# FFN, Q and output matmuls behind a P V block issued as four 32-column tiles, with a planner that follows the tiling mode

## The chip, the cores and the metric

One core of one Trainium2 chip. The metric is the device time of one execution, in microseconds (us), as the median of several runs. "The profile" is one further execution taken by the hardware profiler; its span is the time from the first to the last instruction.

## The reference

A transformer layer on x of 2048 rows by 1024: layer norm, attention with 32 query heads of 32 and a single key/value head, residual; layer norm, gated FFN of width 3584, residual. All in bf16.

```python
q = (xn @ wq).reshape(S, 32, 32); k = xn @ wk; v = xn @ wv      # xn = layernorm(x)
p = softmax(einsum("hqd,kd->hqk", q, k) * 32 ** -0.5)
h = x + (p @ v).reshape(S, 1024) @ wo
g = hn @ w_gate; u = hn @ w_up                                  # hn = layernorm(h)
out = h + (sigmoid(g) * u) @ w_down
```

## The kernel before

**Attention.** Queries are cut into 16 tiles of 128 rows, heads into 8 blocks of four; a "group" G is one query tile with two head blocks (64 groups in all). A *visit* is one group with 256 keys: there are 512, eight a group, 32 a query tile. A visit does S (`emit_S`): eight matmuls of 32 contraction rows by 128, in four row tiles, over 256 columns, into three PSUM banks pairs in turn; then two exps on ScalarE (`ACT Pr L588`), each over 128x1024, which write the P slots of SBUF. After four visits of a group comes half of P V (`mk_PV`, `emit_PV`): 32 matmuls as four column tiles, 128 contraction rows by 32 columns each. The sums of P that softmax divides by are made in one of two ways. For the first four groups (`G < NX`) TensorE multiplies every P slot by ones, 32 more column-tiled matmuls a half. For all others VectorE adds the P slots up into `Ts` (`flush_sums`, L618), merges two halves (L625), and four matmuls with ones close the sum.

**The rest.** Q (`mk_Q`), the output projection (`mk_OP`), gate/up (`mk_GU`, 8 matmuls over 512 columns a group of 512 FFN columns) and down (`mk_D`) use the full 128x128 array. They are cut into single matmuls and stand between the S of two visits. Gate/up ends in a tanh on ScalarE (L860) for the sigmoid, and a multiply on VectorE (L864). Gate/up weights are streamed in pieces of 256 KB through 22 slots (`ring`) over SP's queue; down weights stay in SBUF (`zone`), where x transposed and wq lay before.

**What sets the order.** The kernel is written out by a planner in Python (`Plan`). It holds a free time for each engine and durations for each operation, and issues, one after the other: S as soon as ScalarE's backlog is under 750 ns, a P V block if its inputs are known, else a full matmul from the queues in the order `PRIO`. Where nothing is ready and a PSUM bank is spare, it issues a matmul that only fills the time (`F_ps<-kT,ident`); before visit 0 such matmuls warm up the engine (`S_ps<-hact,ident`). Constants for a change of tiling mode (95, 111, 109 ns) are added to TensorE's free time in `emit_S`, `emit_PV` and the main loop. On the chip each engine runs its own list in order, and semaphores hold it where inputs are late. All matmuls but the transposes come from the helper `mm` and so have one line, L384 in the profile; they are told apart by their tiles: `S_ps<-QTb,kT` is S, `F_ps<-Pr,Vb` P V, `F_ps<-Ts,ones` and `F_ps<-Pr,ones` its sums, `F_ps<-zone` Q, K and V, `F_ps<-wo_sb,OT` output, `F_ps<-ring,hnT` gate/up, `F_ps<-zone,hact` down.

**The start.** x tiles are loaded on SP's queue, wk and wv on ScalarE's. VectorE and GpSimd normalise pairs of x tiles; TensorE transposes the first two, DMAs the others. `TP` is the order of (query tile, FFN slice): slices of tiles 0 and 1 are interleaved by hand, later tiles go through the slices forwards and backwards in turn.

Of the kernel before, what the change touches and what calls it, by code (L numbers as in the profile page):

```python
# [128 lines left out]
def bass_sequential_preLN__grouped_kv_mqa__glu_gated_glu__prompt_kernel(  # L129
# [21 lines left out]
    NI = 2 * NFP  # L151
    TP = [(0, p) for p in range(5)] + [(1, 4), (1, 3), (0, 5), (1, 5), (0, 6), (1, 6)] + [(1, p) for p in (2, 1, 0)]
    TP += [(t, p) for t in range(2, NT) for p in (reversed(range(NFP)) if t % 2 else range(NFP))]
    ITEMS = [(t, p, w) for t, p in TP for w in range(2)]
# [6 lines left out]
    NPS = 16  # L161
    NX = 4
    NB = 3
    NPC = 22
# [8 lines left out]
    with ExitStack() as es:  # L173
# [43 lines left out]
        def xnT(dt, a, n):  # L217
            return xnT4[a // 512][:, dt, a % 512:a % 512 + n]
        wq_sb = zview(DT * S, DT, D)
        o3 = DT * S + DT * D  # L220
# [73 lines left out]
        def load_wq(a, b, deps=()):  # L294
            o = dma(lambda: SP.dma_start(wq_sb[:, :, a * P:b * P], A_wq[:, a * P:b * P].rearrange("(a p) n -> p a n", p=P)),
                    f"wq{a}", D * P * (b - a) * 2, deps, prio=0)
            for g in range(a, b):
                wq_ld[g] = o

        load_x([0])  # L300
        load_x([1])
        wk_ld = dma(lambda: ACT.dma_start(wk_sb, A_wk.rearrange("(a p) j -> p a j", p=P)), "wk", P * DT * DH * 6, prio=0,
                    ring="act")
        wv_ld = dma(lambda: ACT.dma_start(wv_sb, A_wv.rearrange("(a p) j -> p a j", p=P)), "wv", P * DT * DH * 6, prio=0,
                    ring="act")
        load_wq(0, 2)
# [76 lines left out]
        def mm(o, l, r, start, stop, **kw):  # L383
            return lambda: PE.matmul(o, lhsT=l, rhs=r, start=start, stop=stop, **kw)  # L384

# [45 lines left out]
        q_left4 = [2 * NG, 2 * NG, NG, NG]  # L431
        wd_ld = []

        def mk_KV(p):
# [27 lines left out]
        def mk_Q(g, tok, n):  # L462
            def atoms(b):
                return [(mm(F_ps[:, b, 0:n], wq_sb[:, dt, g * P:(g + 1) * P], xnT(dt, tok, n),
                            dt == 0, dt == DT - 1), n, []) for dt in range(DT)]

            def after(b, last):
                q_left[0] -= 1
                q_left4[tok // 512] -= 1
                free_wd(last)  # L470
                early_loads(last)
                if tok == 0:
                    fa, fd = both(QTb[:, :, g, :], F_ps[:, b, 0:256].rearrange("p (a b) -> p a b", a=2))
                    ev = evac(fa, fd, 256, [last], 1)
                    q_ready[0][g] = q_ready[1][g] = ev
                else:
                    k = len(q_store)
                    s = k % NQS
                    deps = [last] + ([q_store[k - NQS]] if k >= NQS else [])
                    fa, fd = both(qst[:, s, 0:n], F_ps[:, b, 0:n])  # L480
                    ev = evac(fa, fd, n, deps, 1)
                    q_store.append(dma(lambda: SP.dma_start(q_dram[:, g, tok:tok + n], qst[:, s, 0:n]),
                                       f"qs{s}", P * 2 * n, [ev], prio=2))
                    for t in range(tok // P, (tok + n) // P):
                        q_of[t].append(q_store[-1])
                        load_q(t)
                return [ev]
            first = lambda: [wq_ld[g]] + [xT_ev[k] for k in range(tok // P, (tok + n) // P)]
            return Group("Q0" if tok == 0 else "Q", atoms, first, after)
# [20 lines left out]
        def free_wd(last):  # L510
            for i in list(wd_left):
                if (i < 4 and q_left4[i] == 0 and 2 * i in k_ev and 2 * i + 1 in k_ev) or \
                        (i >= 4 and q_left[0] == 0 and len(k_ev) == NT // 2):
                    wd_left.remove(i)
                    load_wd(4 * i, 4, [last])
# [39 lines left out]
        def reclaim(v):  # L555
            for sl, own in list(slot_owner.items()):
                if own in pv_done and (own[0] < NX or slot_add.get(sl) is not None):
                    slot_rel[sl] = [pv_done[own], slot_add.get(sl)]
                    del slot_owner[sl]
                    p_free.append(sl)  # L560
            if visits[v][0] >= NX:
                for sl in [sl for sl in p_free if sl >= NPS]:
                    p_free.remove(sl)

        def emit_S(v):
            G, kq = visits[v]
            qb, g = G // ND, 2 * (G % ND)
            deps = s_ready(v)
            pl.free["pe"] += 95.0
            last = None  # L570
            for kk in range(KB):
                for j in range(4):
# [5 lines left out]
                                 deps if (kk == 0 and j == 0) else [], occ=27.4, lat=27.4 + 150.0 + SEM)  # L578
            pl.free["pe"] += 111.0
            for i in range(2):  # L580
# [21 lines left out]
        sum_ev = {}  # L602
        sum_todo = collections.deque((G, kq) for G in range(NX, NT * ND) for kq in range(1, VPG))

        def flush_sums():
            while sum_todo:
                G, kq = sum_todo[0]
                if n_exp_of[G] <= kq or (kq == 1 and G > NX + 1 and (G - 2, 1) not in pv_done):
                    return
                sum_todo.popleft()  # L610
                for i in range(2):
                    T = Ts[:, G % 2, i * 1024:(i + 1) * 1024]
                    ins = [kq - 1, kq] if kq == 1 else [kq]
                    src = [pslot(slot_of[(G, q, i)]) for q in ins]
                    deps = [exp_of[(G, q, i)] for q in ins]
                    deps.append((pv_done.get((G - 2, 1)) if G > NX + 1 else None) if kq == 1 else sum_ev[(G, kq - 1, i)])
                    a, b = (src[0], src[1]) if kq == 1 else (T, src[0])
                    o = pl.op("dve", lambda T=T, a=a, b=b: DVE.tensor_tensor(out=T, in0=a, in1=b, op=ALU.add), deps,  # L618
                              prio=4, **t_dve(1024, 1.92))
                    for q in ins:  # L620
                        slot_add[slot_of[(G, q, i)]] = o
                    sum_ev[(G, kq, i)] = o
# [10 lines left out]
        def mk_PV(G, h):  # L633
            qb, g = G // ND, 2 * (G % ND)

            def block(b):
                r, rs = [], []
                k0, k1 = 8 * h, 8 * h + 8
                for kt in range(k0, k1):
                    kq, kk = kt // KB, kt % KB  # L640
                    for j in range(4):
# [3 lines left out]
                                    kt == k0, kt == k1 - 1, tile_position=(0, DH * j)))  # L645
                        if G < NX:
                            rs.append(mm(F_ps[DH * j:DH * (j + 1), b, 256:512], ones[:, :], pslot(slot)[:, co:co + 256],
                                         kt == k0, kt == k1 - 1, tile_position=(0, DH * j)))
                for j in range(4 if G >= NX and h else 0):
                    r.append(mm(F_ps[DH * j:DH * (j + 1), b, 256:512], ones[:, :],  # L650
                                Ts[:, G % 2, j * 512:j * 512 + 256], True, True, tile_position=(0, DH * j)))
# [46 lines left out]
            def first():  # L698
                r = [exp_of[(G, kq, i)] for kq in range(VPH * h, VPH * (h + 1)) for i in range(2)]
                r += [v_ev.get(p) for p in range(4 * h, 4 * h + 4)]  # L700
                return r + [c_v1] + ([merge_ev.get(G)] if G >= NX and h else [])

# [4 lines left out]
        def emit_PV(t):  # L707
# [8 lines left out]
            b = min(banks, key=lambda b: max([0.0] + [o.end for o in bank_rel[b]]))  # L716
            deps = gr.first() + list(bank_rel[b])
            for fn in gr.atoms(b):
                o = pl.op("pe", fn, deps, occ=27.4, lat=27.4 + 220.0 + SEM)
                o.tag = "PV"  # L720
                deps = []
            pl.free["pe"] += 109.0
            bank_rel[b] = gr.after(b, o)
# [42 lines left out]
        def flush_hT():  # L766
            while late_hT and (late_hT[0] < 2 or (late_hT[0] - 2) in gu_last):
# [4 lines left out]
                for i in range(len(ITEMS)):  # L772
                    if ITEMS[i][0] == t if t > 1 else (ITEMS[i][0] < 2 and t == 0):
                        queues["GU"].append(mk_GU(i))
# [146 lines left out]
        while True:  # L921
# [15 lines left out]
            if sd is None and queues["PV"]:  # L937
                pl.free["pe"] += 95.0
                if emit_PV(t):
                    idle = 0  # L940
                    continue
                pl.free["pe"] -= 95.0
            if cur is not None:
                fn, n, deps, *cb = cur[1][cur_i]
                if known(deps, t) or not can_s:
                    o = pl.op("pe", fn, deps + (cur[2] if cur_i == 0 else []), **t_mm(n))
                    o.tag = cur[0].cls
# [33 lines left out]
            if v == 0 and known([c_id, c_w], t):  # L981
                pl.op("pe", mm(S_ps[:, 5, :], ident[:, :], hact[:, 0:512], True, True), [c_id, c_w], **t_mm(512))
                continue
            idle += 1
            spare = [b for b in range(2) if known(bank_rel[b], t) and (cur is None or b != cur_b)]
            if v and spare:
                pl.op("pe", mm(F_ps[:, spare[0], 0:256], ident[:, :], kT4[:, 0:256], True, True), [k_ev[0]] + list(bank_rel[spare[0]]), **t_mm(256))
                continue
# [108 lines left out]
```

The softmax here doesn't subtract the row's maximum and nothing guards it: scores larger than these inputs give would overflow.

## Time and profile before

| | us |
|---|---|
| median of 6 runs | 1109.46 (1107.73 to 1110.3) |
| the profiled execution, its own time | 1109.09 |
| its span | 1107.0 |
| first S starts, last S starts | 18.86, 1025.80 |

Of the groups of instructions these are the largest on each engine:

| line, engine, tiles | count | busy us, mean ns |
|---|---|---|
| L588 ACT Pr<-S_ps | 1014 | 952.1, 1058 |
| L618 DVE Ts<-Ts,Pr | 720 | 476.3, 681 |
| L384 PE F_ps<-ring,hnT 128x512 | 1754 | 439.7, 381 |
| L384 PE F_ps<-zone,hact 128x512 | 896 | 224.5, 381 |
| L384 PE S_ps<-QTb,kT 32x256 | 4096 | 203.3, 273 |
| L384 PE F_ps<-Pr,Vb 128x256 | 4056 | 134.5, 274 |
| L860 ACT tnh<-F_ps | 112 | 71.7, 640 |

A matmul's length in the profile is a modelled one and overlaps its neighbours; the distance from one start to the next is what it takes of the engine. "PE" is TensorE's matmuls, "PEld" its weight loads, "DVE" VectorE, "ACT" ScalarE, "SP" the DMA queue's engine.

### The profile page before, as it was taken

What the parts mean: (1) busy time and instruction counts of PE and PEld (TensorE: products, weight loads), DVE (VectorE), ACT (ScalarE), POOL (GpSimd) and SP (SyncE); (2) the same over time, 40 slices, a digit from 0 to 9 for tenths busy, and PEclk for the clock granted to TensorE, in tenths of its full rate; (3) what the DMA queues carried; (4) which work ended last, traced back from release to release, by engine and by line L of the source; (5) the groups of instructions that cost most, each with busy time, mean ns of one, the idle gap of its engine ahead of it and who ended that gap; (6) DMA issues with size and microseconds to landing.
All of it is one profiled execution on the core that took longest, in us unless ns stands there. A gap on an engine that the chain in (4) does not pass through costs nothing.

```text
span 1107.0 us, 30139 instructions
## 1 busy us (share of the span) xinstructions
PE 1090.1 (98%) x12306; PEld 475.0 (43%) x12306; DVE 884.7 (80%) x1727; ACT 1012.1 (91%) x1162; POOL 27.9 (3%) x56
## 2 busy tenths in 40 slices
PE   9999999999999999999999999999999999999998
PEld 5664344344344444444444444444444444344443
DVE  7747988798888989798888988898888888888411
ACT  4999999999999999999999999999999999999210
POOL 1100000000000000000000000000000000000000
PEclk9999999999999999999999999999999999999999
DMA  9985499928759595987869495976868595976991
GB/s 238 187 272 173 105 250 283 273 56 233 206 142 251 143 254 134 252 202 182 245 147 248 143 251 146 243 210 186 232 155 241 138 261 150 239 202 169 270 269 44
DMA packets 304730, 222.06 MB, mean 201 GB/s; under 512 B 121552, under 2 KB 295888, under 8 KB 304592
## 3 DMA queue, kind: packets, MB, share of 16 engines
q1 hardware_dynamic: 302512, 220.01, 77.8%
q8 instruction: 97, 1.59, 0.6%
q14 instruction: 41, 0.34, 0.1%
q10 hardware_dynamic: 2080, 0.13, 0.1%
HBM read 189.66 MB, written 7.86 MB: 178 GB/s over the span
## 4 chain that ended last, share of the span: by engine, by line
PE 88%; ACT 4%; DVE 4%; issue 2%; DMA 1%; SPq 0%; POOL 0%; POOLq 0%; DVEq 0%
PE F_ps L384 74%; PE S_ps L384 15%; ACT Pr L588 4%; DMA ring<-in_B_w_gate_dram 1%; DVE st L325 1%; DMA ring<-in_B_w_up_dram 0%; DVE st L323 0%; DVE Ts L618 0%; DVE ring L371 0%; DVE ring L364 0%; ACT tnh L860 0%; DVE hact L274 0%; DVE Rc L680 0%; DVE Oc L668 0%; DVE mv L327 0%
## 5 line engine op out<-in xcount | busy, mean ns | idle before, releaser
L588 ACT ACTIVATE Pr<-S_ps 128x1024 bf16<-128x1024 f32 x1014 | 952.1, 1058 | 6.8 <-PE S_ps L384 6.0
L618 DVE TENSOR_TENSOR Ts<-Ts,Pr 128x1024 bf16<-128x1024 bf16 x720 | 476.3, 681 | 41.2 <-ACT Pr L588 37.4
L384 PE MATMUL F_ps<-ring,hnT 128*128 128x512 bf16 x1754 | 439.7, 381 | 8.1 <-issue 2.2
L384 PEld LDWEIGHTS F_ps<-ring,hnT 128*128 128x128 bf16 x1754 | 149.8, 98 | 221.6 <-issue 79.1
L384 PE MATMUL F_ps<-zone,hact 128*128 128x512 bf16 x896 | 224.5, 381 | 0.0
L384 PE MATMUL S_ps<-QTb,kT 32*128 32x256 bf16 x4096 | 203.3, 273 | 0.2 <-DVE mv L327 0.2
L384 PEld LDWEIGHTS S_ps<-QTb,kT 32*128 32x128 bf16 x4096 | 60.6, 92 | 192.1 <-ACT Pr L588 131.2
L384 PE MATMUL F_ps<-Pr,Vb 128*32 128x256 bf16 x4056 | 134.5, 274 | 0.0
L864 DVE SCALAR_TENSOR_TENSOR hst<-tnh,F_ps 128x512 bf16<-128x512 f32 x112 | 76.7, 684 | 62.7 <-PE F_ps L384 62.7
L384 PEld LDWEIGHTS F_ps<-zone,hact 128*128 128x128 bf16 x896 | 76.2, 98 | 103.8 <-issue 32.4
L384 PEld LDWEIGHTS F_ps<-Pr,Vb 128*32 128x32 bf16 x4056 | 96.8, 96 | 36.7 <-DVE hst L864 10.9
L860 ACT ACTIVATE tnh<-F_ps 128x512 f32<-128x512 f32 x112 | 71.7, 640 | 44.6 <-PE F_ps L384 44.6
L618 DVE TENSOR_TENSOR Ts<-Pr 128x1024 bf16<-128x1024 bf16 x120 | 80.7, 688 | 37.4 <-ACT Pr L588 37.3
L384 PE MATMUL F_ps<-zone 128*128 128x256 bf16 (+2 forms) x576 | 76.2, 276 | 3.7 <-DVE mvb L333 1.0
L384 PE MATMUL F_ps<-wo_sb,OT 128*128 128x512 bf16 x256 | 63.6, 380 | 0.0
L384 PEld LDWEIGHTS F_ps<-zone 128*128 128x128 bf16 x576 | 42.6, 97 | 29.3 <-issue 8.9
L894 DVE SCALAR_TENSOR_TENSOR h_sb<-F_ps,h_sb 128x512 bf16<-128x512 f32 x32 | 22.0, 686 | 35.3 <-PE F_ps L384 35.3
L625 DVE TENSOR_TENSOR Ts<-Ts 128x1024 bf16<-128x1024 bf16 x60 | 41.4, 689 | 1.5
L337 POOL TENSOR_SCALAR zb<-mvb 128x1 bf16<-128x1 bf16 (+1 forms) x24 | 10.5, 439 | 1010.7 <-DVE mvb L333 1010.7
L384 PEld LDWEIGHTS F_ps<-wo_sb,OT 128*128 128x128 bf16 x256 | 22.4, 98 | 29.3 <-issue 6.8
L685 DVE STREAM_TRANSPOSE Rc<-Ri 128x256 f32<-128x256 f32 x64 | 28.3, 442 | 0.1
L668 DVE TENSOR_TENSOR Oc<-F_ps,Oc 128x256 f32<-128x256 f32 x60 | 25.2, 421 | 3.5 <-PE F_ps L384 2.3
(59 smaller groups left out, 350.4 us busy)
## 6 DMA issues: line engine op xcount, KB each, us to landing
ring<-in_B_w_gate_dram SPq DMA_DIRECT2D x308, 256.0 KB, 3.9
ring<-in_B_w_up_dram SPq DMA_DIRECT2D x307, 256.0 KB, 4.1
zone<-in_B_w_down_dram SPq DMA_DIRECT2D x28, 256.0 KB, 4.0
h_sb<-in_A_x_dram SPq DMA_DIRECT2D x16, 256.0 KB, 5.1
out_dram<-h_sb SPq DMA_DIRECT2D x32, 128.0 KB, 2.6
ring<-in_A_x_dram SPq DMA_DIRECT2D x7, 512.0 KB, 6.5
QTb<-q_scratch SPq DMA_DIRECT2D x14, 256.0 KB, 4.4
Pr<-in_B_w_up_dram SPq DMA_DIRECT2D x9, 256.0 KB, 3.8
```

Source lines behind the costliest of these rows:

```text
L325: b = pl.op("dve", lambda k=k, src=src: DVE.bn_stats(st[:, k, 1, :], src[:, 512:1024]), dep, prio=prio, occ=590, lat=756, order=[st_user.g ...
L337: f = pl.op("pool", lambda: POOL.tensor_scalar(out=zb[:, ph, sl].unsqueeze(2), in0=mvb[:, ph, sl, 1:2], scalar1=LN_EPS_BF16, scalar2=None, ...
L384: return lambda: PE.matmul(o, lhsT=l, rhs=r, start=start, stop=stop, **kw)
L588: exps[u] = pl.op("act", lambda slot=slot, pb=pb: ACT.activation(out=pslot(slot).rearrange("p (a b) -> p a b", a=2), in_=S_ps[:, pb:pb + 2 ...
L618: o = pl.op("dve", lambda T=T, a=a, b=b: DVE.tensor_tensor(out=T, in0=a, in1=b, op=ALU.add), deps, prio=4, **t_dve(1024, 1.92))
L625: merge_ev[G] = pl.op("dve", lambda T4=T4: DVE.tensor_tensor(out=T4[:, :, 0, :], in0=T4[:, :, 0, :], in1=T4[:, :, 1, :], op=ALU.add), [sum ...
L668: a = pl.op("dve", lambda: DVE.tensor_tensor(out=Oc[:, :], in0=O, in1=Ob, op=ALU.add), [last, oc_ev[G], o_ev.get(G - 1)], prio=0, **t_dve( ...
L685: d = pl.op("dve", lambda: DVE.transpose(out=Rc[:, :], in_=Ri[:, :].unsqueeze(2).to_broadcast([P, 2 * P // DH, DH])), [r], prio=2, **t_dve ...
L860: tanh_of[n] = pl.op("act", lambda: ACT.activation(out=tnh[:, n % 2, :], in_=F_ps[:, b, :], func=ACTF.Tanh, scale=0.5), [last, tn_user.get ...
L864: e = pl.op("dve", lambda: DVE.scalar_tensor_tensor(out=hst[:, n % NST, :], in0=tnh[:, n % 2, :], scalar=1.0, in1=F_ps[:, b, :], op0=ALU.a ...
L894: e = pl.op("dve", lambda: DVE.scalar_tensor_tensor(out=h_sb[:, t % 4, sl], in0=F_ps[:, b, :], scalar=0.5, in1=h_sb[:, t % 4, sl], op0=ALU ...
```

## The change

The planner keeps the tiling mode that TensorE is in (`mode`), and adds the drain where the mode changes (`enter`). A full matmul that comes while the mode is still that of P V goes out as four column tiles, up to `NCR` = 12 of them after one P V block:

```diff
+    NCR = 12
         def mm(o, l, r, start, stop, **kw):
-            return lambda: PE.matmul(o, lhsT=l, rhs=r, start=start, stop=stop, **kw)
+            fn = lambda: PE.matmul(o, lhsT=l, rhs=r, start=start, stop=stop, **kw)
+            if not kw:
+                fn.col = lambda: [mm(o[DH * j:DH * (j + 1)], l[:, DH * j:DH * (j + 1)], r, start, stop,
+                                     tile_position=(0, DH * j)) for j in range(4)]
+            return fn
+        mode = ["full"]
+        col_run = [0]
+        DRAIN = {"full": 96.0, "row": 92.0, "col": 100.0}
+        def enter(m):
+            if mode[0] != m:
+                pl.free["pe"] += DRAIN[mode[0]]
+                mode[0] = m
+                col_run[0] = 0
+        def emit_mm(fn, n, deps):
+            if mode[0] == "col" and hasattr(fn, "col") and col_run[0] < NCR:
+                col_run[0] += 1
+                for f in fn.col():
+                    o = pl.op("pe", f, deps, occ=n / 9.6 + 1.2, lat=n / 9.6 + 171.0 + SEM)
+                    deps = []
+                return o
+            enter("full")
+            return pl.op("pe", fn, deps, **t_mm(n))
...
-                    o = pl.op("pe", fn, deps + (cur[2] if cur_i == 0 else []), **t_mm(n))
+                    o = emit_mm(fn, n, deps + (cur[2] if cur_i == 0 else []))
```

`emit_S` calls `enter("row")` and adds 18 in place of 95 and 111; `emit_PV` calls `enter("col")` and adds 9 in place of 109.

The second half of the first four groups has its sums made by VectorE, as the later groups have:

```diff
-                        if G < NX:
+                        if h == 0 and G < NX:
                             rs.append(mm(F_ps[DH * j:DH * (j + 1), b, 256:512], ones[:, :], pslot(slot)[:, co:co + 256],
...
-                for j in range(4 if G >= NX and h else 0):
+                for j in range(4 if h else 0):
...
+        def k_first(G):
+            return VPH if G < NX else 0
-        sum_todo = collections.deque((G, kq) for G in range(NX, NT * ND) for kq in range(1, VPG))
+        sum_todo = collections.deque((G, kq) for G in range(NT * ND) for kq in range(k_first(G) + 1, VPG))
```

The order of FFN slices, the start and the loads:

```diff
-    TP = [(0, p) for p in range(5)] + [(1, 4), (1, 3), (0, 5), (1, 5), (0, 6), (1, 6)] + [(1, p) for p in (2, 1, 0)]
-    TP += [(t, p) for t in range(2, NT) for p in (reversed(range(NFP)) if t % 2 else range(NFP))]
+    TP = [(t, p) for t in range(NT) for p in (reversed(range(NFP)) if t % 2 else range(NFP))]
...
-        wk_ld = dma(lambda: ACT.dma_start(wk_sb, A_wk.rearrange("(a p) j -> p a j", p=P)), "wk", P * DT * DH * 6, prio=0,
-                    ring="act")
+        wk_ld = dma(lambda: ACT.dma_start(wk_sb, A_wk.rearrange("(a p) j -> p a j", p=P)), "wk", P * DT * DH * 6, [x_ld[1]], prio=0, ring="act")
...
-                pl.op("pe", mm(S_ps[:, 5, :], ident[:, :], hact[:, 0:512], True, True), [c_id, c_w], **t_mm(512))
+                pl.op("pe", mm(S_ps[:, 5, :], ident[:, :], hact[:, 0:512], True, True), [c_id, c_w],
+                      **t_mm(512 if t > 5200.0 else 1024))
...
-                        (i >= 4 and q_left[0] == 0 and len(k_ev) == NT // 2):
+                        (i in (4, 5) and all(q_done[g] == S for g in range(4 * i - 16, 4 * i - 12))) or \
+                        (i == 6 and len(k_ev) == NT // 2):
```

wv waits for `x_ld[1]` like wk; wq lies in two halves (`wq2`) in place of one piece, so that down weights can take the place of a half when its four head blocks are done. `reclaim` keeps P slots of the first groups' second halves until VectorE has added them.

## The prediction

> **What bounds the kernel now.** First the page: busy shares, and the chain of waits.
>
> ```profile
> span 1107.0 us, 30139 instructions
> PE 1090.1 (98%) x12306; PEld 475.0 (43%) x12306; DVE 884.7 (80%) x1727; ACT 1012.1 (91%) x1162; POOL 27.9 (3%) x56
> ...
> PE 88%; ACT 4%; DVE 4%; issue 2%; DMA 1%; SPq 0%; POOL 0%; POOLq 0%; DVEq 0%
> ```
>
> TensorE is never free, and the chain is 88% TensorE. ScalarE is close behind, so the second question is how much TensorE can gain before ScalarE sets the pace. A busy share does not tell what one matmul or one change of tiling mode costs, because matmuls overlap; their starts do. So next the timeline of PE (start, length, group):
>
> ```profile
> 594.17 1.47 PE L384 MATMUL F_ps<-zone,hact 128*128 128x512 bf16 x6
> 595.57 0.40 PE L384 MATMUL S_ps<-QTb,kT 32*128 32x256 bf16 x8
> 595.90 1.06 PE L384 MATMUL F_ps<-Pr,Vb 128*32 128x256 bf16 x32
> 596.78 0.28 PE L384 MATMUL F_ps<-Ts,ones 128*32 128x256 bf16 x4
> 597.00 0.61 PE L384 MATMUL F_ps<-zone,hact 128*128 128x512 bf16 x2
> ...
> 619.78 1.06 PE L384 MATMUL F_ps<-Pr,Vb 128*32 128x256 bf16 x32
> 620.77 0.40 PE L384 MATMUL S_ps<-QTb,kT 32*128 32x256 bf16 x8
> ...
> 630.20 2.12 PE L384 MATMUL F_ps<-ring,hnT 128*128 128x512 bf16 x9
> 632.25 0.40 PE L384 MATMUL S_ps<-QTb,kT 32*128 32x256 bf16 x8
> ```
>
> From start to start, nine full matmuls and the change to S take 632.25 - 630.20 = 2.05 us; six take 595.57 - 594.17 = 1.40. A full matmul over 512 columns is therefore (2.05 - 1.40)/3 = 0.217 us, and the change 1.40 - 6 x 0.217 = 0.10. P V's 32 matmuls are eight rounds of four column tiles: (596.78 - 595.90)/8 = 0.110 us a round. S is two rounds, 0.22, and takes 0.33 until P V starts: 0.11 for the change. P V to full (596.78 to 597.00, one round) and P V to S (619.78 to 620.77, eight rounds) cost 0.11 too. Every change of mode, whatever the pair, is 0.10 to 0.11 us; I use 0.105.
>
> Then ScalarE's timeline, for its own pace:
>
> ```profile
> 591.10 1.02 ACT L588 ACTIVATE Pr<-S_ps 128x1024 bf16<-128x1024 f32 x1
> 592.00 0.61 ACT L860 ACTIVATE tnh<-F_ps 128x512 f32<-128x512 f32 x1
> 592.48 13.89 ACT L588 ACTIVATE Pr<-S_ps 128x1024 bf16<-128x1024 f32 x15
> ```
>
> An exp that need not wait takes 0.90 us to the next start, a tanh 0.48; in the run of 15 the mean step is (13.89 - 1.02)/14 = 0.92, so exps wait a little for S. A tile of 128 query rows is 32 visits (64 exps) and 7 tanhs: at least 64 x 0.90 + 7 x 0.48 = 61.0 us.
>
> Last the busy times by stretch (length, then PE, PEld, DVE, ACT, POOL, clock, DMA share, GB/s): visits 0 to 31, of these visits 16 to 31, then visits 32 to 63, a later tile, and the time after the last S.
>
> ```profile
> 18.86:88.00 69.14, 66.15 (x1130) 45.61 (x1133) 41.97 (x119) 63.62 (x78) 5.75 (x12) 1.00 0.94 228
> 57.00:88.00 31.00, 30.55 (x568) 20.03 (x570) 11.64 (x29) 30.22 (x33) 0.00 (x0) 1.00 0.89 279
> 88.00:149.20 61.20, 59.76 (x731) 24.95 (x731) 58.33 (x114) 60.23 (x67) 1.52 (x2) 1.00 0.51 149
> 339.50:402.20 62.70, 62.59 (x717) 25.93 (x720) 53.68 (x103) 62.62 (x72) 1.14 (x2) 1.00 0.80 207
> 1025.90:1107.00 81.10, 77.18 (x418) 34.55 (x413) 20.20 (x37) 8.37 (x13) 0.79 (x2) 1.00 0.74 194
> ```
>
> From about 340 us each tile takes 62.53 us (the same three down matmuls of the pattern start at 593.10 and, a tile on, at 655.63). The last 81 us hold no S: TensorE works off what is left there, so each FFN matmul that is fitted in earlier shortens the end by 0.217 us. The clock is 1.00 throughout.
>
> **The change part by part.** Counts of the changed kernel are from the order of its instructions as built, set against before.
>
> *The column tiles.* 159 matmuls become four tiles each: 11 Q, 5 output, 43 gate/up, 100 down. Most runs are one or two matmuls long (71 of 80), because the next S is due then. The trace has no four tiles that stream one and the same 512 columns; P V streams four different pieces of 256. Lower bound 0.217: a round of P V (0.110) costs what 256 full columns would (0.108). Upper bound 0.87, the four one after another. I take 0.217: P V has the same tiles, weight shape and rate, and only the shared stream is new.
>
> A rule of the Trainium skill speaks against this part (TensorEngine Tiling (Array Packing), Restrictions and Gotchas): column tiling excludes fast weight load. The profile's groups give a 128x32 load 96 ns and a 128x128 load 98, and four of the former go by within a 110 ns round. If four loads stood in a row, 0.38 us, 159 matmuls would lose 26 us by that reading; by the row they lose nothing.
>
> *Changes of mode.* 1169 before, 1094 after: 75 fewer, 7.9 us. S, P V, two matmuls, S needs two changes where it needed three.
>
> *Work removed.* 112 row-sum matmuls of the first four head groups (28 rounds, 3.1 us) and 24 of 32 idle-filling matmuls over 256 columns (24 x 0.108 = 2.6 us). VectorE gets 24 adds and 4 merges in their place, 28 x 0.67 (476.3 us for 720 adds in the groups) = 18.8 us, nearly all in visits 16 to 31. There it was busy 11.64 of 31 us: the 19.4 free ones hide them, just. Where they don't, the evacuations behind them on VectorE come late, and then TensorE's next bank; I allow 0 to 3 us.
>
> *Visits 0 to 159.* Changes fall by 19 (2.0 us); with the removed 5.7 that is 7.7, of which 16 more full matmuls use 3.5: TensorE's own sum falls by 4.2. But its rows for visits 32 to 63 now add up to 56.2 us, and ScalarE needs 64 x 0.90 + 3 x 0.48 = 59.0 (58.6 before, when the stretch took 61.2). With the same excess over ScalarE it takes 61.6. So the bounds of these 160 visits are -4.2 and, with VectorE, +3; I take +0.5, by the row of ScalarE, busy 60.23 of 61.20.
>
> *Later tiles.* Both kernels do 184 full matmuls, 64 rounds of S and 68 of P V a tile; changes fall from 74 to 69. Before: 184 x 0.217 + 132 x 0.110 + 74 x 0.105 = 62.2 us, 62.53 measured. After, 0.53 less: 62.0, still above ScalarE's 61.0. Eleven such stretches: -5.8. If exps' waits eat half, -2.9.
>
> *After the last S.* 342 full matmuls before; 302 and 24 column-tiled after: 16 fewer, and two changes fewer: -(16 x 0.217 + 0.2) = -3.7. These are the 16 done in the first 160 visits.
>
> *The start.* Warm-up matmuls before the first transposes fall from 40 to 28.
>
> ```profile
> 1.68 10.42 PE L384 MATMUL S_ps<-hact,ident 128*128 128x512 bf16 x40 [1.68 <-POOL ident L278]
> ...
> 8.46 0.88 DVE L371 TENSOR_SCALAR ring<-ring,rstd 128x1024 bf16<-128x1024 bf16 x2
> ...
> 11.93 1.06 PE L389 MATMUL F_ps<-ident,ring 128*128 128x128 bf16 x16
> ```
>
> The transposes' input is ready at 8.46 + 0.88 = 9.34; they start 2.6 us later, behind the warm-up. Twelve fewer end it near 9.5: up to 2.4 us. wk and wv now wait for the second x tile (its statistics start by 5.2) on ScalarE's queue, with only the evacuation after the transposes behind them; landing some 3.5 us after issue, they are there before K's matmuls (14.8 before). But up to 45.6 us VectorE works without a gap on layer norm, which starts no earlier: bounds -2.4 and 0; I take half, -1.2.
>
> The new order of FFN slices has 656 weight loads for 633, 0.26 MB each. At the 269 GB/s of the stretch 149 to 214 us that is 23 x 0.97 = 22 us of transfer on SP's queue, in the first three tiles; later tiles have 40 in both. I cost it at nothing: 41 in tile 1 take 40 us, and TensorE spends 26 visits, 51 us, on that tile. Without this cover it is up to 22.
>
> *Sum:* -1.2 + 0.5 - 5.8 - 3.7 = -10.2 us. The profiled execution took 1109.09 (span 1107.0 and 2.1 around it), 0.4 under the median of 1109.46: 1109.5 - 10.2 = 1099.3.
>
> **Rivals.** *ScalarE paces all visits:* TensorE's gain becomes waiting for exps. For it: 91% busy, 4% of the chain. Against: 62.53 a tile against 61.0. Only the end gains: 1109.5 - 3.7 = 1105.8. *TensorE's sum is all:* nothing is eaten early: -2.4 - 4.2 - 5.8 - 3.7 = -16.1, 1093.4. Against: ScalarE's 59.0 in visits 32 to 63. *Column-tiled matmuls are dearer* because four tiles pull the same columns of ring, zone or wo_sb: if two go at a time, 0.434, then 159 x 0.217 = +34.5, 1133.8. Against: P V's rounds at full rate. It decides from 10.2/159 = 0.064 over, 0.281 a round. *The change does little:* the weights of the first tiles come late and eat 10 of the 22 us, about 1109.5. Against: the cover above.
>
> **How the numbers follow.** This forecast 0.50, its own range 1095 to 1104 (start, early visits and half the steady gain at their ends); all of TensorE's sum 0.15; ScalarE's pace 0.15; dearer tiles 0.10; late weights 0.10. I predict 1099.3, and 1093 to 1106 holds the first three. 0.2%, 2.2 us, is about what a measurement of this kernel can tell from no change. Faster: the first three, 0.80. Late weights spread over both sides of no change: 0.07 same, 0.03 slower; with dearer tiles 0.13 slower.
>
> **What would show it.** Rounds of four over 512 columns start 0.217 us apart, and their change to S costs 0.105. A later tile takes 62.0 us. The first S starts near 16.5 us. Visit 160 starts within 2 us of 339.5 less the gain at the start. After the last S some 77 us remain. It would be wrong if rounds take over 0.28, if a tile stays at 62.5, if TensorE waits for weights between 130 and 260 us, or for VectorE between 55 and 90.

## The result, and the profile after

The changed kernel takes 1106.41 us (median of 20 runs, 1102.49 to 1111.64) where the kernel before takes 1109.65 in its 45 runs. The ratio is 0.9975, 95% interval 0.9967 to 0.9983: faster by 3.2 us, by more than the 0.2% that can be told from no change, but a third of the 10.2 that were forecast and 0.4 us outside the range.

The clock that TensorE was granted has a part in this. In most executions of the changed kernel it was halved for one to three stretches of 3.4 us. By the traces one stretch gives a mean clock of 0.998 and two give 0.997; 0.995 is then three. Of its 21 executions (the profiled one counted) six had the full clock, with a median of 1104.67; ten had one stretch (1106.41), three had two (1109.10) and two had three (1110.77). The kernel before had the full clock in its profile and in 64 of the 67 executions that stand beside the experiments with their clocks.

Stage by stage, from the starts of S in the profiled executions (us; the forecast in the last column):

| stage | before | after | change | forecast |
|---|---|---|---|---|
| until the first S | 18.86 | 21.33 | +2.5 | -1.2 |
| visits 0 to 159 | 320.65 | 322.20 | +1.6 | +0.5 |
| visits 160 to 511 | 686.28 | 684.26 | -2.0 | -5.8 |
| last S to the end | 81.24 | 75.90 | -5.3 | -3.7 |
| span | 1107.03 | 1103.70 | -3.3 | -10.2 |

The page of the changed kernel, its span, busy times and chain of waits:

```profile
span 1103.7 us, 30884 instructions
PE 1078.5 (98%) x12635; PEld 473.3 (43%) x12635; DVE 901.4 (82%) x1753; ACT 1010.1 (92%) x1164; POOL 32.1 (3%) x56
...
PE 55%; ACT 22%; DVE 12%; issue 6%; DMA 4%; POOL 0%; SPq 0%; ACTq 0%; DVEq 0%
```

TensorE's share of the span is the same 98%, but its share of the chain went from 88% to 55%: the chain now leaves TensorE often, for an exp or for a step of VectorE. A busy share alone would have hidden that.

TensorE's timeline at the same place of the pattern (start, length, group):

```profile
597.01 0.40 PE L382 MATMUL S_ps<-QTb,kT 32*128 32x256 bf16 x8
597.34 1.06 PE L382 MATMUL F_ps<-Pr,Vb 128*32 128x256 bf16 x32
598.22 0.28 PE L382 MATMUL F_ps<-Ts,ones 128*32 128x256 bf16 x4
598.33 0.60 PE L382 MATMUL F_ps<-zone,hact 128*32 128x512 bf16 x8
598.87 0.40 PE L382 MATMUL S_ps<-QTb,kT 32*128 32x256 bf16 x8
```

The eight matmuls of 128x32 weights are two down matmuls cut into four. They begin one round of the sums (598.33 - 598.22 = 0.11) after them, so there is no change of mode in front. With the change to S they take 598.87 - 598.33 = 0.54 = 2 x 0.217 + 0.105. A round of four tiles over 512 columns costs what a full matmul costs.

The busy times of the stretches that the prediction showed of before (visits 0 to 31, of these 16 to 31, 32 to 63, a later tile, the time after the last S; PE, PEld, DVE, ACT, POOL, clock, DMA share, GB/s):

```profile
21.33:90.46 69.13, 65.62 (x1031) 44.84 (x1031) 51.50 (x130) 63.40 (x80) 4.43 (x9) 1.00 0.88 232
59.00:90.46 31.46, 30.75 (x478) 18.84 (x471) 26.16 (x55) 30.96 (x35) 0.00 (x0) 1.00 0.90 279
90.46:151.47 61.01, 57.55 (x748) 24.25 (x749) 58.38 (x117) 60.47 (x68) 2.44 (x2) 1.00 0.60 182
343.50:405.90 62.40, 62.14 (x741) 25.95 (x738) 53.85 (x103) 62.40 (x72) 1.50 (x2) 1.00 0.73 201
1027.90:1103.70 75.80, 72.88 (x474) 33.84 (x470) 19.68 (x36) 7.68 (x12) 0.79 (x2) 0.99 0.82 218
```

VectorE in visits 16 to 31 went from 11.64 to 26.16 us with the moved sums, and the 32 visits took 69.13 us where they took 69.09: in this execution the free time did hide them. In two others of the same order up to visit 160 (the runs with short exps and short adds below) they took 69.58 and 71.53, the latter with a stretch of half clock in it. In visits 32 to 63 TensorE fell to 57.55 us busy and ScalarE stayed at 60.47 of 61.01, the bound that the prediction set there. The later tile fell by little.

The start and the later tiles are furthest from the forecast, by 3.7 and 3.8 us. TensorE, and ScalarE with its queue, in the first 22 us of the changed kernel:

```profile
10.42 1.06 PE L411 MATMUL F_ps<-ident,ring 128*128 128x128 bf16 x16
...
13.25 1.91 PE L382 MATMUL F_ps<-zone 128*128 128x256 bf16 x16
...
18.05 3.35 PE L382 MATMUL F_ps<-zone 128*128 128x256 bf16 x31 [2.67 <-DMA zone<-in_A_wv_dram]
```

```profile
4.02 0.43 ACTq L302 DMA_DIRECT2D zone<-in_A_wk_dram  x1
4.49 0.70 ACTq L303 DMA_DIRECT2D zone<-in_A_wv_dram  x1
...
11.06 1.94 ACT L273 ACTIVATE zone<-F_ps 128x1024 bf16<-128x1024 bf16 x2 [8.85 <-PE F_ps L411]
14.37 1.34 ACT L313 ACTIVATE zone<-zone 128x256 bf16<-128x256 bf16 x4 [1.36 <-DMA zone<-in_A_wk_dram]
```

The transposes did start 1.5 us earlier (10.42 against 11.93). But wk, issued at 4.02, lands only at 14.3 (the copy that reads it starts at 14.37), and wv, issued at 4.49, keeps TensorE standing for 2.67 us until 18.05. K's matmuls stand in one group with V's (`mk_KV`), and the group waits for wv, though K itself needs only wk. The copy of wk (L315 before) ran at 4.23 in the kernel before, 3.5 us after its issue.

Behind this wait the clock is halved: the busy times from 17.39 to 20.81 us (columns as above, the clock before the DMA share), and the same matmuls in another execution of this order, where the clock stayed full (the run with short exps):

```profile
17.39:20.81 3.42, 2.75 (x28) 2.06 (x29) 3.39 (x13) 0.40 (x2) 0.93 (x2) 0.50 1.00 217
```

```profile
16.87 2.20 PE L382 MATMUL F_ps<-zone 128*128 128x256 bf16 x31 [2.42 <-DMA zone<-in_A_wv_dram]
```

The 31 matmuls take 3.35 us at half clock and 2.20 at the full one, so 1.15 us of the +2.5 are the clock. The first S there came at 19.00.

### The profile page after: what moved, and what is told of

Its sections match the earlier page's. It is cut to its first block, busy times and chain, and to the rows that moved or that the text cites. A ratio compares the mean times of both kernels' runs of the same rounds, so it can differ in the third digit from the quotient of the medians.

```text
span 1103.7 us, 30884 instructions
## 1 busy us (share of the span) xinstructions
PE 1078.5 (98%) x12635; PEld 473.3 (43%) x12635; DVE 901.4 (82%) x1753; ACT 1010.1 (92%) x1164; POOL 32.1 (3%) x56
## 4 chain that ended last, share of the span: by engine, by line
PE 55%; ACT 22%; DVE 12%; issue 6%; DMA 4%; POOL 0%; SPq 0%; ACTq 0%; DVEq 0%
PE F_ps L382 47%; ACT Pr L613 21%; PE S_ps L382 8%; DVE Ts L647 7%; DMA ring<-in_B_w_gate_dram 1%; DMA zone<-in_A_wv_dram 1%; ACT tnh L891 1%; DVE Rc L709 1%; DVE hst L895 1%; DVE Oc L697 1%; DVE h_sb L777 1%; DMA zone<-ring 0%; DVE st L321 0%; DMA hact<-hst 0%; DVE st L323 0%
## 5 line engine op out<-in xcount | busy, mean ns | idle before, releaser
L647 DVE TENSOR_TENSOR Ts<-Ts,Pr 128x1024 bf16<-128x1024 bf16 x732 | 484.5, 680 | 48.7 <-ACT Pr L613 45.9
L382 PE MATMUL F_ps<-ring,hnT 128*128 128x512 bf16 (+1 forms) x1889 | 444.0, 381 | 11.6 <-issue 4.0
L382 PEld LDWEIGHTS F_ps<-ring,hnT 128*128 128x128 bf16 (+1 forms) x1889 | 149.9, 97 | 219.7 <-issue 73.4
L382 PE MATMUL F_ps<-zone,hact 128*32 128x512 bf16 (+1 forms) x1196 | 221.8, 380 | 0.5 <-DMA hact<-hst 0.5
L382 PEld LDWEIGHTS F_ps<-zone,hact 128*32 128x32 bf16 (+1 forms) x1196 | 79.9, 97 | 96.8 <-issue 20.6
L647 DVE TENSOR_TENSOR Ts<-Pr 128x1024 bf16<-128x1024 bf16 x126 | 84.8, 684 | 33.7 <-ACT Pr L613 33.6
L382 PE MATMUL F_ps<-zone 128*128 128x256 bf16 (+3 forms) x609 | 76.7, 284 | 5.7 <-DMA zone<-in_A_wv_dram 2.7
L382 PE MATMUL F_ps<-wo_sb,OT 128*128 128x512 bf16 (+1 forms) x271 | 63.7, 381 | 0.1
L382 PEld LDWEIGHTS F_ps<-zone 128*128 128x128 bf16 (+1 forms) x609 | 44.6, 98 | 29.0 <-issue 10.4
L382 PEld LDWEIGHTS F_ps<-wo_sb,OT 128*128 128x128 bf16 (+1 forms) x271 | 21.4, 97 | 29.5 <-issue 6.8
```

Source lines behind the costliest of these rows:

```text
L382: fn = lambda: PE.matmul(o, lhsT=l, rhs=r, start=start, stop=stop, **kw)
```

## The experiments

"In the same order" means that the kernel is planned as the changed one is and the one edit is made to the finished lists, so that each engine runs its instructions in the same sequence; "planned anew" means that the planner saw the edit and wrote another order. Stage figures are of one profiled execution each. In one and the same order with the late wk and wv the first S comes at 19.00 and 19.42 us where the clock stayed full, and at 20.90 and 21.33 where it was halved just before, so the start alone is read to about 1 us. From visit 160 to the last S no profile has a halved clock. "A later tile" is a tenth of the time from visit 160 to visit 480.

### Single parts, planned anew

The loads of wk and wv without their wait:

```diff
-        wk_ld = dma(..., P * DT * DH * 6, [x_ld[1]], prio=0, ring="act")
-        wv_ld = dma(..., P * DT * DH * 6, [x_ld[1]], prio=0, ring="act")
+        wk_ld = dma(..., P * DT * DH * 6, prio=0, ring="act")
+        wv_ld = dma(..., P * DT * DH * 6, prio=0, ring="act")
```

> The changed kernel, but wk and wv no longer wait for the second x tile. In the changed kernel TensorE stood 2.7 us for wv at 18.05 us and the first S started at 21.33 (18.86 before). Theory 'late wv': first S at 17 to 18.5 us, visit 160 some 3 us earlier than in the changed kernel, total near 1103.4. Rival 'layer norm on VectorE bounds the first 50 us anyway': first S earlier all the same, but visit 160 within 1 us of the changed kernel's, total 1105.5 to 1106.5.

Median 1106.85, ratio to the kernel before 0.998 (0.9971 to 0.999). The first S came at 17.47 and visit 160 at 336.17, 7.4 us earlier than with the wait. All of it was lost again, most behind the last S, 83.37 us against 75.90: the new order leaves 326 full matmuls there, not 302 (and 24 in tiles in both). The time does not tell the theories apart, since two things changed; the start does.

No column tiles outside P V:

```diff
-    NCR = 12
+    NCR = 0
```

> The changed kernel with NCR = 0, so no matmul but those of P V runs in column tiles; all else stays. By starts and counts of its order TensorE's own sum is 7.4 us longer (4.4 in visits 0 to 159, 4.5 in later visits, 1.5 shorter after the last S). Theory 'TensorE's sum sets the time': 1113 to 1114, a tile 0.2 to 0.4 longer. Rival 'ScalarE and TensorE are so close that each visit takes the longer of the two': visits change by less than half of that and the end gains 1.5, total 1105.5 to 1109.

Median 1103.98, ratio 0.9954 (0.9942 to 0.9966): without the tiles that it is named for, the change brings more, some 5.1 us by the ratio. A later tile takes 62.31 us, the end 75.14.

The tiles alone: the kernel before with `NCR = 12` and the mode accounting.

```diff
+    NCR = 12
...
-            pl.free["pe"] += 95.0
+            enter("row")
...
-                    o = pl.op("pe", fn, deps + (cur[2] if cur_i == 0 else []), **t_mm(n))
+                    o = emit_mm(fn, n, deps + (cur[2] if cur_i == 0 else []))
```

> The kernel before with the column tiles and the mode-following planner alone: order of slices, start, loads and sums as before. TensorE's own sum falls by 9.4 us against before (2.8 in visits 0 to 159, 8.3 in later visits, the end 1.7 longer). Theory 'TensorE's sum': 1100 to 1101, a tile at 62.0. Rival 'each visit takes the longer of the two': a tile at 62.2 to 62.4, total 1106 to 1110.

Median 1110.32, ratio 1.0014 (1.0003 to 1.0025): no gain. A later tile takes 62.35, the end 83.60.

### What holds a later tile

Exps over 896 of 1024 columns from visit 160 on, in the same order:

```diff
-                    ... in_=S_ps[:, pb:pb + 2, :], ...
+                    ... in_=S_ps[:, pb:pb + 2, 0:ne], ...    # ne = 448 if v >= 160 else 512
```

> The changed kernel, same order on every engine; from visit 160 on each exp covers 896 of its 1024 columns (128 columns of P are left as they were), so ScalarE has some 0.11 us less to do per exp, 6.8 us per tile. Theory 'ScalarE holds TensorE up in the visits': a tile falls from 62.34 to 61.5 to 61.8, total near 1099. Rival 'TensorE stands for other reasons (PSUM banks, weights, transposes)': a tile stays within 0.15 of 62.34, total 1104.5 to 1106.5.

Median 1104.33, ratio 0.9954 (0.9938 to 0.9971). The exps' row in the groups, of the changed kernel and of this one (busy us, mean ns | idle before, and what ended most of it):

```profile
L613 ACT ACTIVATE Pr<-S_ps 128x1024 bf16<-128x1024 f32 x1014 | 953.4, 1081 | 7.5 <-PE S_ps L382 7.5
```

```profile
L613 ACT ACTIVATE Pr<-S_ps 128x896 bf16<-128x896 f32 (+1 forms) x1014 | 897.7, 971 | 52.5 <-PE S_ps L382 46.0
```

ScalarE's freed time turned into waiting for S, and a later tile went from 62.38 to 62.24 us. An eighth off the exps brings 0.14 us of a tile, not the half of the gain that I had allowed ScalarE.

The same order with the four tiles issued as one full matmul:

```diff
-                for f in fn.col():
-                    o = pl.op("pe", f, deps, occ=n / 9.6 + 1.2, lat=n / 9.6 + 171.0 + SEM)
-                    deps = []
-                return o
+                q = n / 9.6 + 1.2
+                return pl.op("pe", fn, deps, occ=4 * q, lat=3 * q + n / 9.6 + 171.0 + SEM)
```

> The changed kernel in its own order on every engine, but the 159 column-tiled matmuls are issued as full ones at the same places. 80 more changes of mode: by 0.105 us each TensorE's own sum is 8.3 us longer (2.5 in visits 0 to 159, 0.5 a tile later, 0.2 at the end). Theory 'the column tiles do save this, and what was lost was lost elsewhere': 1113 to 1115, a tile 0.4 to 0.5 longer. Rival 'the saved time only turns into waits for PSUM banks': a tile less than 0.25 longer, total 1106.5 to 1110.

Median 1112.40, ratio 1.0031 (1.0022 to 1.004), 6.0 us over the changed kernel. A later tile takes 62.77 us for 62.38. It has 80 changes of mode more, 8.4 us at 0.105 each, and about 70% of it reaches the end. At equal clock it is less: 4.7, 3.4 and 4.0 us between the executions with one, two and three stretches of half clock, and 11 x 0.39 = 4.3 by the tiles. So in the order planned for them the tiles save half or more of what they are meant to save.

This run also parts the order from the tiles. It does the work of the kernel before in a later tile, 184 full matmuls and 74 changes of mode, and takes 62.77 us for 62.53: the new order alone costs 0.24 us a tile. The tiles then save 0.39 of the 0.53 forecast, and 0.15 us of gain is left.

Yet the planner's own order without tiles does the same work with nearly as many changes (1167 for 1174) in 8.4 us less: the order counts for more than the tiles.

VectorE's adds over half the columns from visit 160 on, in the same order:

```diff
-                    ... DVE.tensor_tensor(out=T, in0=a, in1=b, op=ALU.add), deps,
+                    ... DVE.tensor_tensor(out=T[:, 0:ne], in0=a[:, 0:ne], in1=b[:, 0:ne], op=ALU.add), deps,
```

> The changed kernel in its own order; from visit 160 on VectorE's adds for the row sums cover 512 of their 1024 columns (half of the sums is left out), some 0.27 us less each, 3.5 us or more per tile. Theory 'in the later tiles TensorE stands because VectorE gives the PSUM bank of P V back late': a tile falls from 62.38 to 61.8 to 62.1, total 1101 to 1104.5. Rival 'the waits have another cause': a tile stays above 62.25, total 1105.5 to 1106.5.

Median 1102.54, ratio 0.9945 (0.9928 to 0.9961); a later tile 62.18 us, 0.20 less. VectorE counts for about as much as ScalarE. The two add up to 0.34 us, near the 0.38 by which a tile's time beyond TensorE's own sum grew (62.2 and 62.53 before, 61.7 and 62.38 after, by the prediction's prices). But they were not run together, nor on the kernel before, so that they explain this growth is not shown.

What is waited for shows in the waits of TensorE's weight loads between 400 and 960 us, nine tiles (total us, times, longest; part of these waits lies beside matmuls that still run). The kernel before, the changed one, the changed one's order with full matmuls in place of the tiles, and the one planned without column tiles:

```profile
PEld F_ps L384 <- DVE hst L864: 7.9, 27, 0.4
PEld F_ps L384 <- ACT tnh L860: 7.6, 18, 0.4
PEld F_ps L384 <- DVE Rc L685: 1.9, 9, 0.2
```

```profile
PEld F_ps L382 <- ACT tnh L891: 11.5, 27, 0.4
PEld F_ps L382 <- DVE Rc L709: 8.8, 18, 0.6
PEld F_ps L382 <- DVE hst L895: 3.9, 17, 0.2
```

```profile
PEld F_ps L382 <- ACT tnh L889: 11.0, 26, 0.4
PEld F_ps L382 <- DVE Rc L707: 8.0, 18, 0.6
```

```profile
PEld F_ps L382 <- ACT tnh L891: 3.8, 9, 0.4
PEld F_ps L382 <- DVE Rc L709: 1.8, 5, 0.4
```

Rc is VectorE's last read of a P V block's PSUM bank; the bank is free for the next group only then. The waits for tnh and Rc are nearly the same with full matmuls in place of the tiles (11.0 and 8.0 us for 11.5 and 8.8): they belong to the order that the planner wrote for the tiles, not to the tiles. The wait for hst, the multiply behind the tanh, fell meanwhile, from 7.9 to 3.9. One place of the changed kernel, TensorE's and VectorE's lines; behind this P V block stands S, and no tiles:

```profile
646.34 1.06 PE L382 MATMUL F_ps<-Pr,Vb 128*32 128x256 bf16 x32
...
647.08 0.69 DVE L647 TENSOR_TENSOR Ts<-Ts,Pr 128x1024 bf16<-128x1024 bf16 x1 [0.71 <-ACT Pr L613]
...
647.68 0.42 DVE L697 TENSOR_TENSOR Oc<-F_ps,Oc 128x256 f32<-128x256 f32 x1
...
648.02 0.44 DVE L709 STREAM_TRANSPOSE Rc<-F_ps 128x256 f32<-128x256 f32 x1
...
648.56 0.59 PE L382 MATMUL F_ps<-ring,hnT 128*128 128x512 bf16 x2 [0.19 <-issue]
```

The sums of P V (four matmuls at 647.22) are done near 647.5, but VectorE has an add of Ts in hand until 647.77; then Oc and Rc take until 648.46, and the gate/up matmul behind them starts at 648.56. The wait is labelled "issue" here; TensorE's list waits at this place for VectorE's semaphore, and 0.1 us after Rc it goes on, so it is the bank.

### The start

The wait taken out in the same order, by one line behind the planner's last step:

```diff
         pl.drain()
+        wk_ld.deps, wv_ld.deps = [], []
```

> The changed kernel in its own order on every engine, only the wait of wk's and wv's DMA for the second x tile is gone. Theory 'late wv': the first S moves from 21.3 to 17 to 18.5 us, and visit 160 comes 2.5 to 4 us earlier, total 1102.5 to 1104. Rival 'layer norm and the loads of x bound the first stretch': first S earlier, visit 160 within 1 us, total 1105.5 to 1106.5.

Median 1102.18, ratio 0.994 (0.9928 to 0.9952), 4.2 us under the changed kernel. At equal clock it is 2.8 us (the full clock, two executions against six) and 2.5 (one stretch of half clock, three against ten). Its TensorE and ScalarE lines:

```profile
15.30 2.20 PE L382 MATMUL F_ps<-zone 128*128 128x256 bf16 x31
17.43 0.40 PE L382 MATMUL S_ps<-QTb,kT 32*128 32x256 bf16 x8
```

```profile
0.86 0.43 ACTq L302 DMA_DIRECT2D zone<-in_A_wk_dram  x1
...
12.97 1.33 ACT L313 ACTIVATE zone<-zone 128x256 bf16<-128x256 bf16 x4
```

wk and wv land 4.2 and 6.1 us after their issue. The group of K and V starts at 15.30, with no wait, for 18.05, and takes 2.20 us for 3.35; visit 160 starts at 338.76 for 343.53, and at 344.30 and 344.64, with more half clock before it, in the two other profiles that share the changed kernel's order and loads up to there. By stage against the kernel before: the first S -1.4, visits 0 to 159 +0.7, later visits -2.0, the end -4.6. The first two are the forecast's -1.2 and +0.5.

Without the tiles and without the wait: `NCR = 0` and the line above.

> No column tiles outside P V (NCR = 0, 1103.98 measured), and in that order the wait of wk and wv for the second x tile is gone. If the two add up: 1100 to 1101.5. If the start is bounded by layer norm: 1103 to 1104.

Median 1100.99, ratio 0.9925 (0.9913 to 0.9937): the fastest of all, ahead of both kernels.

### The end, and the accounting

The changed kernel with `NCR = 0`, and in one run the row sums of the first four groups given back to TensorE, in the other the slices of tiles 0 and 1 interleaved as before:

```diff
-                        if h == 0 and G < NX:
+                        if G < NX:
...
-                for j in range(4 if h else 0):
+                for j in range(4 if G >= NX and h else 0):
```

```diff
-    TP = [(t, p) for t in range(NT) for p in (reversed(range(NFP)) if t % 2 else range(NFP))]
+    TP = [(0, p) for p in range(5)] + [(1, 4), (1, 3), (0, 5), (1, 5), (0, 6), (1, 6)] + [(1, p) for p in (2, 1, 0)]
+    TP += [(t, p) for t in range(2, NT) for p in (reversed(range(NFP)) if t % 2 else range(NFP))]
```

> No column tiles outside P V, and the sums of the first four groups back on TensorE. By the built order 354 full matmuls stand behind the last S (323 with the sums on VectorE, both without column tiles). Theory 'the short end comes from work fitted in early, for which the sums have to leave TensorE': the time from the last S goes from 75 back to 81 to 83 us, total 1108 to 1111. Rival 'VectorE's extra adds cost as much early as they save at the end': visits 0 to 159 fall by 4 us or more, total within 1.5 of 1104.

> No column tiles outside P V, and the order of FFN slices as before (tiles 0 and 1 interleaved). By the built order 52 filling matmuls for 8, and 354 full ones behind the last S for 323. Theory 'the plain order of slices finds work earlier': end back to 81 to 83 us, total 1108 to 1111. Rival 'its 23 more weight loads hold up the first tiles': without them visits 64 to 159 are 3 us or more shorter, total 1103 to 1106.

Medians 1114.47 (1.0046, 1.0033 to 1.006) and 1110.24 (1.0014, 1.0005 to 1.0022). Either leaves 354 full matmuls behind the last S for 323, and the end takes 82.91 and 83.00 us for 75.14. The short end needs both parts together (75.14 with both, 82.37 with neither, in the next run).

The accounting alone, the kernel before with it and `NCR = 0`:

> The kernel before with the planner's mode accounting alone (no column tiles, nothing else). TensorE's own sum is that of before (1076.9 for 1077.1), 354 matmuls behind the last S for 342. Theory 'accounting alone only shifts work between the visits and the end': 1108.5 to 1110.5. Rival 'honest accounting makes an order that waits less': a tile at 62.2 to 62.3, total 1105.5 to 1107.5.

Median 1108.58, ratio 0.9994 (0.9982 to 1.0005), no change; a later tile 62.50, the end 82.37. Against it the tiles alone (1110.32) lose 1.7 us.

### Fewer tiles, and VectorE again

At most two tiled matmuls behind a P V block, without the wait for wk and wv: `NCR = 2` and the line above.

> The changed kernel with NCR = 2 in place of 12, and without the wait of wk and wv. By counts TensorE's own sum is 2.5 us under the changed kernel's, a tile's at 61.27 (61.46), and no run of twelve behind the last S. Theory 'the sum of a tile sets it': a tile at 62.0 to 62.2, total 1097.5 to 1100. Rival 'waits for banks take it back': a tile at 62.3 to 62.4, total 1100 to 1102.5.

Median 1118.95, ratio 1.0088 (1.0076 to 1.01): slower than the kernel before, although TensorE's own work for a later tile, added up from its counts, is the least of all (61.27 us for the changed kernel's 61.46 by the expectation's prices; by the prediction's 61.5, where before is 62.2 and after 61.7). The tile takes 64.19. TensorE's waits in its nine tiles from 400 to 960 us, and one of the places:

```profile
PE F_ps L382 <- DVE Rc L709: 8.2, 9, 0.9
PE F_ps L382 <- DMA ring<-in_B_w_gate_dram: 5.6, 10, 1.0
```

```profile
696.30 0.39 PE L382 MATMUL F_ps<-ring,hnT 128*32 128x512 bf16 x4
696.49 0.69 DVE L647 TENSOR_TENSOR Ts<-Ts,Pr 128x1024 bf16<-128x1024 bf16 x1 [0.22 <-ACT Pr L613]
...
697.10 0.42 DVE L697 TENSOR_TENSOR Oc<-F_ps,Oc 128x256 f32<-128x256 f32 x1
697.43 0.44 DVE L709 STREAM_TRANSPOSE Rc<-F_ps 128x256 f32<-128x256 f32 x1
...
697.93 0.60 PE L382 MATMUL F_ps<-ring,hnT 128*128 128x512 bf16 x2 [0.91 <-DVE Rc L709]
```

The add of Ts got in front of Oc and Rc, and TensorE stands 0.91 us, once in each tile. The same kernel with VectorE's adds halved from visit 160 on:

> The kernel with at most two column-tiled matmuls after a P V block and no wait for wk and wv (1118.95 measured, a tile 64.19 us though TensorE's own sum is 61.27), same order on every engine; from visit 160 on VectorE's adds for the row sums cover 512 of their 1024 columns, which leaves half of the sums out. Theory 'VectorE's adds keep the PSUM bank of P V from being read, and TensorE stands for it': a tile falls by 0.7 us or more, to 63.5 or less, total 1108 to 1112. Rival 'weights or exps hold TensorE there': a tile stays within 0.3 of 64.19, total 1116 to 1119.

Median 1114.52, ratio 1.0047 (1.0032 to 1.0063), 4.4 us under the run before; a later tile 63.71. TensorE's waits:

```profile
PE F_ps L382 <- DVE Rc L710: 5.8, 9, 0.6
PE F_ps L382 <- DMA ring<-in_B_w_gate_dram: 3.5, 6, 0.9
```

The add in front of the read-out is a part of it: halved from 0.69 to 0.42 us, it takes 0.3 us off the longest of these waits. 0.6 us, once in each tile, remain. What the rest is, what is left of the add, the read-out's own length or the later weights, these runs do not settle.

## Why the prediction was right or wrong

**The start (+2.5 for -1.2).** The step that failed is "landing some 3.5 us after issue, there before K's matmuls". I took the time to land from an issue at 0.72, ahead of most other loads. At 4.02 the loads of wk and wv stand beside those of x and wq, issued from 0.72 on, with the 16 DMA engines busy for 0.98 of the first 17 us, and took 10.3 and 13.4 us. Taking that wait alone away gave 4.2 us back, shown in the same order; 2.5 to 2.8 of it at equal clock. The rest, by this estimate some 1.5 us, goes with the half clock, which the prediction did not have at all. In the traces of all runs each of the 13 stretches of half clock before the last microseconds starts in, or less than 3.4 us after, a time of 1.56 us or more in which TensorE stood; the kernel before, once started, never stands for more than 1.05. Nine other times of 1.54 to 2.42 us were not followed by one. So a wait like that for wv can cost twice, and does so in some executions only. That the standing brings the half clock is read from these traces; no run was made to test it. A page of the Trainium skill, "DMA: Bandwidth & Descriptors", section "Issuing engines are not separate DMA queues", says that transfers issued from different engines share the same 16 DMA engines and interleave; the 10.3 us agree with it. I had counted what is queued behind wk on ScalarE, and not what is ahead of it in the DMA engines. That the transposes would start earlier was right. "VectorE works without a gap" was not: before, it stands 2.38 us until 19.51. But the -1.4 of the run without the wait lies within the bounds that I took from it.

**Later tiles: the work fell as said, the time did not (-2.0 for -5.8).** The cost of the tiles (0.217 for a round, no change of mode in front) was right, and by the counts TensorE's own work fell by the 0.53 us a tile that were forecast. But what a tile takes beyond this work rose from 0.3 to 0.7 us, and a tile takes 62.38, nearer to the 62.5 named as a sign of being wrong than to 62.0. The step that failed is the sum itself, "still above ScalarE's 61.0": it held TensorE against ScalarE's pace, took the waits of the old order to hold for the new one, and gave them no term. Measured, the new order costs 0.24 us a tile with the same work, and the tiles save 0.39 of 0.53 in it. Neither short exps (-0.14) nor short adds (-0.20) give the tile its gain alone; ScalarE as the pace of the later visits is refuted by the first. That the new order waits more for VectorE's read-out of the P V bank (8.8 and 8.0 us for 1.9) is seen in the waits; that these waits are the whole of the missing 0.4 us is not shown.

**Tiles against no tiles.** I took the tiles for the source of the steady gain. Held in one order they save 6.0 us (3.4 to 4.7 at equal clock); but in each of three pairs the planner's order without them was the faster, by 2.4, 1.2 and 1.7 us (each a difference of two medians; the intervals against the kernel before overlap or nearly touch). Between executions with one stretch of half clock, two to ten of each kernel, it is 3.8, 3.2 and 0.5, so the clock does not make the difference. By stage, all three pairs lose in the later visits (1.0, 0.6 and 0.2 us) and behind the last S (0.8, 2.3 and 1.2). Why the orders with tiles come out worse I saw only as these waits, and in the third pair, with the kernel before's order of slices, a later tile is even shorter with them (62.35 for 62.50): the cause stays open. The planner's durations do not foresee them, or it would have avoided a tile of 64.19 us.

**Early visits (+1.6 for +0.5).** In the profile the moved sums were hidden by VectorE's free time, and ScalarE was the bound in visits 32 to 63 by its busy time (60.47 of 61.01), both as said; no run tests the latter. Between 55 and 90 us TensorE waits for VectorE once, 0.7 us. With the start mended the stage is +0.7.

**The end (-5.3 for -3.7).** In the two stretches after the last S, TensorE is busy for 77.18 of 81.10 us before and for 72.88 of 75.80 after: 4.3 of it is work, where 16 matmuls and two changes were put at 3.7, and 1.0 is idle time that the new end does not have (before, TensorE waits there 0.6 us for Rc and 0.2 for weights, after not at all). This was only read, not tested. In the three other profiles of this order with tiles the end is 75.87 to 76.59. It was tested that the moved sums and the plain order of slices bring the short end together, not the tiles.

**The rivals.** Dearer tiles are refuted by the 0.54 us above. The time, 1106.4, fell near the forecast of the rival with ScalarE as the pace (1105.8) by chance, for other reasons: that rival had no loss at the start, and short exps leave the tile as it is. Late weights between 130 and 260 us cost TensorE 3.0 us of waits, and 1.0 before: this sign of being wrong did show, by 2.0 us, and the cover that I named held for most of the 22.

## What to carry to other kernels

A load that is moved by a few microseconds at the start must be costed against everything that is in flight when it is issued, whichever queue it has. A wait that lets TensorE stand for some microseconds must be costed together with the clock behind it, and runs are best set against runs with the same granted clock. Where a planner writes the order, an edit that saves time in a fixed order may still lose it in the new one: test it in the order held fixed and planned anew, and switch off the part that the change is named for. A sum of an engine's own work is a bound, not a forecast, once another engine must read its PSUM banks before it can go on, and a new order has waits of its own.

## What was not expected of the hardware

A load of 64 KB in 64-byte pieces took 3.5 us when issued at 0.72 us, and 10.3 and 13.4 us when issued at 4.02 and 4.49. With the wait the time also scatters more, 1102.5 to 1111.6 in 20 runs and 1101.7 to 1104.0 in five without it, which are few; at the full clock the runs with the wait lie between 1102.5 and 1105.8. A stretch of half clock lasts 3.4 us (twice that in one trace), and each further one goes with some 1.7 to 2.7 us in the medians of the changed kernel. Four column tiles that stream the same 512 columns run at the full rate, 0.217 us a round; four that stream different 256 columns take 0.110.
